# An attention and MLP block on one core: a look-ahead in TensorE's order, and 33 groups of scores on VectorE in place of 34

## The chip, the cores and the metric

The kernel runs on one core of a Trainium2 chip. The metric is the device time of one execution in microseconds. The kernel before takes 461.35 us, the median of three runs (460.85 to 461.57). The profiled execution took 461.18 us; its span from the first to the last instruction is 459.3 us.

## What is computed

Two branches share a layer norm of `x` (2048 rows of 448 values), and their product is added to `x`:

```python
x = A_x
xn = _layernorm(x, axis=-1)
s = _A_ref(xn, A_wqkv, A_wo)          # attention: 16 heads of 28, all 2048 x 2048 scores
g = _silu(_B_ref(xn, B_w1, B_b1, B_w2, B_b2))   # MLP: 448 -> 1792, gelu, -> 448
return x + s * g
```

with the attention's core

```python
scores = jnp.einsum("bhqd,bhkd->bhqk", q, k) * scale
p = _softmax(scores, axis=-1)
o = jnp.einsum("bhqk,bhkd->bhqd", p, v)
```

The softmax needs 16 x 2048 x 2048 exponentials, some 67 million[...]. Most of the kernel is there to keep ScalarE at them.

## The kernel before

**Tiles.** The scores are cut into 1024 tiles of 128 keys by 512 queries of one head. Tile number m belongs to block m // 64 (four heads by 512 queries: 16 blocks) and to head m % 4 of the block. A head's 28 values, padded to 32, fill 32 of the 128 rows of TensorE's array, so up to four score matmuls of different heads run side by side, each in its own row group (`t_score`, L1223). Each writes one PSUM bank of 512 float32 values.

**Units and ScalarE.** ScalarE takes the scores in units: three banks and two banks in turn (two and two in the first block), from the two ends of a ring of banks. `p_scores` makes the scores of unit u once the exp of unit u - 2 has ended (its banks are free then), and `p_exps` (L1279) runs one exp over a unit's banks and writes bfloat16 to slots of a buffer P (18 slots; the page also names them `h` and `xnT`, since in some stretches free parts of these tiles serve as slots). A slot is free once the PV matmuls that read its old content have run.

**Groups on VectorE.** `QUADS` lists groups of four tiles (group q is tiles 4q to 4q + 3) whose exponential VectorE computes in place of ScalarE: four evictions from PSUM as scaled 16-bit integers (`p_apass`, L1382), then five operations over all four tiles that make the powers of two by integer and polynomial arithmetic (`p_expq`, L1433 to L1440). The scores of such tiles are made in banks of their own when one is free, or joined to the matmuls of the next unit (`may_join`, `join`) so that the row groups are filled. Tiles in `QUADS` never reach ScalarE. Their PV work takes twelve matmuls a group where ScalarE's needs four.

**PV and the rest.** `pv_task` (L1494) multiplies eight tiles, and VectorE's groups that are ready, into one accumulator bank; at the end of each block `p_epi` copies it out and divides by the sums. Beside this TensorE has the projections of q, k and v (L744, L1031), the MLP's first product (L1089), its second (L1158), the output product (L1591), and small dummy matmuls (`p_busy`, L905) that keep its clock up when it has little to do. Early in block 9 ScalarE does the GELU in one stretch (L1138) after a change of its table; the exps go on before and after. Later, as the MLP's second product is done chunk by chunk, it takes five tanh for the silu (L1173, L1189).

**What sets the order.** Every engine's order is made before the launch, in Python. All work is split into tasks with an engine, the buffers read and written, a planned length (`dur`, `lat`) and a priority. `run` goes through them as a list scheduler: it works out when each next task could start (`start_of`, from the planned ends of what it needs), takes the one that can start first, and among those of the same engine within 0.1 us of it the one of the best priority. The task is then put at the end of its engine's order, with semaphore waits on what it needs. On the chip each engine runs its list in order. So a task that the planner puts ahead of a unit's scores stays ahead of them on the chip, whatever ScalarE is doing by then. Scores have a priority of 1, other work 1.2 to 6, dummies 95; but a task that can start now is taken before scores that can start in 0.2 us.

The choice in the code before is this:

```python
            s0, p0 = min(cand, key=lambda c: (c[0], c[1][3].prio, c[1][0], c[1][1]))
            E = p0[3].E
            near = [c for c in cand if c[1][3].E == E and c[0] <= s0 + EPS]
            s, p = min(near, key=lambda c: (c[1][3].prio, c[1][0], c[0], c[1][1]))
```

Of the kernel before, what the change touches and what calls it, by code (L numbers as in the profile page):

```python
# [11 lines left out]
PE, ACT, DVE, POOL, SP = ET.PE, ET.Activation, ET.DVE, ET.Pool, ET.SP  # L12
# [15 lines left out]
MTOT = NBLK * T * 4  # L28

GM = 64 * 9 + 6  # L30
QUADS = (17, 22, 25, 36, 37, 59, 65, 72, 82, 87, 99, 103, 115, 122, 129, 135, 138, 142, 152, 153, 157, 158, 164, 168, 178, 180, 194, 199, 211, 213, 222, 229, 234, 242)
SM_SCALE = DH ** -0.5
LOG2E = 1.4426950408889634
EXP_A3, EXP_A2, EXP_LC = 0.16391228, 0.00783292, 1.1187538523466403
# [12 lines left out]
SEM, OWN = 0.07, 0.03  # L47
SWITCH = 0.1
JOINT = 0.05
LEAD, WAIT, GLEAD = 0, 3.0, 48  # L50
EPS = 0.1

# [24 lines left out]
class _Kernel:  # L77
# [132 lines left out]
    def run(self):  # L210
        idle = 0
        while True:
            self.settle()
            if not self.procs:
                return
            cand = []
            for p in self.procs:
                if isinstance(p[3], _Task):
                    s = self.start_of(p[3])
                    if s is not None:  # L220
                        cand.append((s, p))
            if not cand and idle < 100:
                idle += 1
                self.now += 0.1
                continue
            if not cand:
                raise RuntimeError("stuck at %.1f: %s" % (self.now, [(p[0], p[3] if not isinstance(p[3], _Task) else "task") for p in self.procs][:20]))
            s0, p0 = min(cand, key=lambda c: (c[0], c[1][3].prio, c[1][0], c[1][1]))
            E = p0[3].E
            near = [c for c in cand if c[1][3].E == E and c[0] <= s0 + EPS]  # L230
            s, p = min(near, key=lambda c: (c[1][3].prio, c[1][0], c[0], c[1][1]))
            if E == PE and p[3].prio >= 90:
                soon = [c for c in cand if c[1][3].E == PE and c[1][3].prio < 90 and c[0] <= s + p[3].dur]
                if soon:
                    s, p = min(soon, key=lambda c: (c[0], c[1][3].prio))
            idle = 0
            self.now = max(self.now, s)
            self.put(p[3], s)
            self.advance(p)

    def ready(self, toks, ahead=0.0):
        return all(b.tw is not None and b.tw <= self.now + ahead for b in toks)

    def build(self):
        nc = self.nc
        with self.es:
            for E, nm in ((PE, "ev_pe"), (ACT, "ev_act"), (DVE, "ev_dve"), (POOL, "ev_pool"), (SP, "ev_sp")):
                self.evsem[E] = self.sem(nm)
                self.evcnt[E] = 0
            self.alloc()  # L250
            self.schedule()
            block = self.es.enter_context(nc.Block())
            for E, attr in ((SP, "sync"), (POOL, "gpsimd"), (DVE, "vector"), (ACT, "scalar"), (PE, "tensor")):
                lst = self.prog[E]

                def run(eng, lst=lst):
                    for f in lst:
                        f(eng)
                getattr(block, attr)(run)
# [127 lines left out]
    def schedule(self):  # L387
# [27 lines left out]
        K.pv_done = [False] * MTOT  # L415
        K.late = {4 * q + k for q in QUADS for k in range(4)}
        K.late_left = [sum(1 for q in QUADS if K.sub_of(4 * q) == b) for b in range(NBLK + 3)]
        K.late_on = False
# [907 lines left out]
    def may_join(self, r):  # L1326
# [7 lines left out]
        st = K.start_of(p["task"])  # L1334
        return st is not None and max(r["tok"].tr, r["tok"].tw or 0.0) + SEM <= st + JOINT

# [15 lines left out]
    def p_late(self):  # L1352
        K = self
        yield ("until", lambda: K.late_on)
        K.spawn(K.p_room(), 0)
        for q in QUADS:
            m0 = 4 * q
# [49 lines left out]
    def assign(self, ms, b0):  # L1407
        K = self
        n = len(ms)
        runs = [list(range(i, i + n)) for i0, w in K.pon for i in range(i0, i0 + w - n + 1)]  # L1410
        run = min(runs, key=lambda x: (max(K.plast.get(i, -1) for i in x), x[0]))
        for i, m in zip(run, ms):
            K.PB[m] = i
            K.PPREV[m] = K.plast.get(i)
            K.plast[i] = m
        K.units.append((ms, b0, run[0]))
# [266 lines left out]
```

## Time and profile before

| engine | busy, us | share of 459.3 us |
|---|---|---|
| ScalarE | 446.8 | 97% |
| TensorE | 436.3 | 95% |
| VectorE | 373.1 | 81% |
| GpSimd | 40.9 | 9% |

ScalarE's time is made up of these groups (the count, the mean from a record's start to its end, and the sum):

| what | count | mean, ns | busy, us |
|---|---|---|---|
| exp of three banks (1536 columns), into P, `h` or `xnT` | 165 | 1503 to 1518 | 248.9 |
| exp of two banks (1024 columns) | 196 | 1073 to 1099 | 208.1 |
| exp of one bank (512 columns), the last | 1 | 636 | 0.6 |
| GELU of 1024 to 2560 columns | 17 | 1037 to 2333 | 27.3 |
| tanh of 448 to 1792 columns | 5 | 614 to 1766 | 7.2 |

The sums of the first two rows alone are more than the span: records of neighbouring exps overlap, and the page's busy time counts an overlap once. So a record's mean is longer than the time that one more of its kind would add, and the distance between the starts of two neighbours is the better measure of both a price and a delay. The span has four stages: the layer norm and the first projections up to the first exp at 12.9 us, exps up to 247 us, the GELU up to 276 us, exps again up to the start of the last one at 452.2 us, and the end.

### The profile page before, as it was taken

The page shows a single profiled execution, that of the slowest core. Times are in us where ns is not written, and L with a number is a line of the kernel's source. Part 1 is how long each engine was busy: PE and PEld are TensorE (multiplying, and loading weights), DVE is VectorE, ACT ScalarE, POOL GpSimd, SP SyncE. Part 2 cuts the span into 40 slices and gives each one's busy share as a digit, 9 for nine tenths or more (in the row PEclk, how much of TensorE's full clock was granted, in tenths as well). Part 3 has the DMA queues.
Part 4 walks back from the last instruction along what each step waited for, and adds up shares of the span by engine and source line. Part 5 has one row for each costly group of instructions (what it writes and reads, how often), then busy time and mean ns, then how long its engine had stood idle before and what let it go on. Part 6 is the DMA issues. An engine that isn't in the chain of part 4 may idle for free.

```text
span 459.3 us, 10615 instructions
## 1 busy us (share of the span) xinstructions
PE 436.3 (95%) x4431; PEld 162.2 (35%) x4431; DVE 373.1 (81%) x584; ACT 446.8 (97%) x408; POOL 40.9 (9%) x85
## 2 busy tenths in 40 slices
PE   6999999999999999999999999999999999989994
PEld 5543333333332323323333333333323334343452
DVE  8956898894897798878989989847778978999965
ACT  5999999999999999999999999999999999999994
POOL 7470000000000000000000000000000100101111
PEclk9999999999999999999999999999999999999998
DMA  8701000000000000000050000000000001300331
GB/s 269 268 2 37 2 0 1 1 1 4 1 1 0 1 2 3 1 2 1 0 143 1 2 0 2 1 1 0 1 1 2 1 0 42 43 1 1 42 43 41
DMA packets 8050, 11.16 MB, mean 24 GB/s; under 512 B 1698, under 2 KB 6994, under 8 KB 7955
## 3 DMA queue, kind: packets, MB, share of 16 engines
q1 hardware_dynamic: 6850, 8.43, 6.1%
q0 software_dynamic: 864, 1.38, 2.4%
q8 instruction: 35, 0.57, 0.5%
q10 hardware_dynamic: 288, 0.69, 0.4%
q14 instruction: 13, 0.10, 0.1%
HBM read 8.61 MB, written 3.21 MB: 26 GB/s over the span
## 4 chain that ended last, share of the span: by engine, by line
PE 47%; ACT 38%; issue 11%; DVE 3%; POOL 1%; ACTq 0%; DVEq 0%; POOLq 0%
ACT P L1279 18%; PE ring L1223 13%; ACT xnT L1279 9%; ACT h L1279 9%; PE acc L1494 8%; PE ring L1089 5%; PE ring L1158 3%; PE misc L1158 3%; PE acc L905 3%; PE misc L1089 2%; PE misc L744 2%; PE ring L744 2%; PE acc L887 1%; PE misc L1223 1%; PE ring L1031 1%
## 5 line engine op out<-in xcount | busy, mean ns | idle before, releaser
L1279 ACT ACTIVATE P<-ring 128x1024 bf16<-128x1024 f32 (+1 forms) x188 | 217.6, 1265 | 1.4 <-PE ring L1223 1.0
L1223 PE MATMUL ring<-qT,kT 32*128 32x512 bf16 (+2 forms) x1074 | 145.1, 358 | 11.4 <-ACT P L1279 5.6
L1279 ACT ACTIVATE h<-ring 128x1024 bf16<-128x1024 f32 (+1 forms) x102 | 117.8, 1268 | 0.2
L1223 PEld LDWEIGHTS ring<-qT,kT 32*128 32x128 bf16 x1074 | 37.6, 91 | 134.2 <-ACT P L1279 55.7
L1279 ACT ACTIVATE xnT<-ring 128x1536 bf16<-128x1536 f32 (+1 forms) x72 | 83.4, 1308 | 0.0
L1494 PE MATMUL acc<-P,vaug 128*32 128x512 bf16 (+2 forms) x524 | 49.2, 358 | 0.0
L1089 PE MATMUL ring<-xnT,w 128*128 128x512 bf16 x156 | 41.4, 382 | 1.1 <-ACT h L1138 0.9
L1564 POOL CAST rhi<-rc 128x16 bf16<-128x16 f32 x15 | 6.0, 400 | 365.2 <-DVE rc L1562 297.0
L905 PE MATMUL acc<-ident,zero 128*128 128x128 bf16 x393 | 34.3, 221 | 0.0
L1223 PE MATMUL misc<-qT,kT 32*128 32x512 bf16 (+1 forms) x78 | 29.1, 376 | 0.0
L905 PEld LDWEIGHTS acc<-ident,zero 128*128 128x128 bf16 x393 | 22.3, 97 | 18.8 <-issue 18.2
L1494 PE MATMUL acc<-h,vaug 128*32 128x512 bf16 x248 | 27.6, 384 | 0.0
L1158 PE MATMUL misc<-w,h 128*128 128x448 bf16 x112 | 27.3, 356 | 0.0
L1158 PE MATMUL ring<-w,h 128*128 128x448 bf16 x112 | 27.2, 355 | 0.0
L1382 DVE TENSOR_SCALAR x_sb<-misc 128x512 uint16<-128x512 f32 x31 | 21.3, 686 | 6.2 <-PE misc L1223 5.9
L1089 PE MATMUL misc<-xnT,w 128*128 128x512 bf16 x68 | 19.5, 383 | 0.5 <-DVE qT L1581 0.5
L1552 DVE CAST E_sb<-acc 128x512 bf16<-128x512 f32 x15 | 10.4, 690 | 11.7 <-PE acc L1494 11.7
L1494 PE MATMUL acc<-xnT,vaug 128*32 128x512 bf16 (+2 forms) x240 | 18.7, 330 | 0.9 <-ACT P L1279 0.7
L1089 PEld LDWEIGHTS ring<-xnT,w 128*128 128x128 bf16 x156 | 12.1, 97 | 20.0 <-issue 7.2
L1494 PEld LDWEIGHTS acc<-P,vaug 128*32 128x32 bf16 x524 | 11.8, 94 | 15.0 <-issue 11.8
L1382 DVE TENSOR_SCALAR kT<-ring 128x512 uint16<-128x512 f32 x19 | 13.1, 688 | 4.3 <-PE ring L1223 3.4
L1138 ACT ACTIVATE h<-h 128x2048 bf16<-128x2048 bf16 (+2 forms) x8 | 16.2, 2029 | 0.0
(269 smaller groups left out, 663.2 us busy)
## 6 DMA issues: line engine op xcount, KB each, us to landing
w<-in_B_w_dram SPq DMA_DIRECT2D x1, 1568.0 KB, 7.6
w<-in_B_w_dram SPq DMA_DIRECT2D x1, 1344.0 KB, 8.6
out_dram<-in_A_x_dram SPq DMA_DIRECT2D x3, 448.0 KB, 10.7
out_dram<-h POOLq DMA_DIRECT2D x6, 224.0 KB, 3.9
x_sb<-in_A_x_dram SPq DMA_DIRECT2D x2, 448.0 KB, 5.0
h<-in_A_wqkv_dram SPq DMA_DIRECT2D x3, 168.0 KB, 5.1
x_sb<-in_A_x_dram ACTq DMA_DIRECT2D x1, 448.0 KB, 4.4
h<-in_A_x_dram SPq DMA_DIRECT2D x1, 448.0 KB, 4.3
```

What stands on the lines that cost most here:

```text
L744: ins = eng.matmul(bank, w[:, kt, g * 128:(g + 1) * 128], K.xnT[:, kt, c * 512:(c + 1) * 512], start=(kt == 0), stop=(kt == KT - 1))
L887: yield _Task(PE, lambda eng: eng.matmul(bank[:, 0:256], K.ident[:, :], K.E_sb[:, 0, 0:256], start=True, stop=True), [K.b_id, K.b_pads], [ ...
L905: ins = eng.matmul(K.acc[:, 0:128], K.zero[:, :], K.ident[:, :], start=False, stop=True, skip_group_check=True)
L1089: ins = eng.matmul(bank, K.w1[:, kt, ft * 128:(ft + 1) * 128], K.xnT[:, kt, c * 512:(c + 1) * 512], start=(kt == 0), stop=(kt == KT - 1))
L1138: yield _Task(ACT, lambda eng, dst=dst, src=src: eng.activation(dst, src, ACTF.Gelu_apprx_tanh), rd, wr, 0.4267 * n + (0.1 if pc else 0.06 ...
L1158: ins = eng.matmul(ps, hv[:, ft, t * 128:(t + 1) * 128], K.w2[:, ft, :], start=(ft == 0), stop=(ft == FT - 1))
L1223: return eng.matmul(dst, K.kT[32 * j:32 * j + 32, g, t * 128:(t + 1) * 128], K.qT[32 * j:32 * j + 32, g, c * 512 + q0:c * 512 + q0 + nq], ...
L1279: return eng.activation(reg[:, i0:i0 + n, :], K.ring[:, b0:b0 + n, :], ACTF.Exp, scale=SM_SCALE)
L1382: yield _Task(DVE, lambda eng: eng.tensor_scalar(K.unit[u][:, 512 * k:512 * k + 512].bitcast(dt.uint16), bank, SM_SCALE * LOG2E * 128.0, ( ...
L1494: return eng.matmul(K.acc[32 * j:32 * j + 32, q0:q0 + nq], K.vaug[:, t, 4 * g + j, :], ap[:, col:col + nq], tile_position=(0, 32 * j), sta ...
L1552: yield _Task(DVE, lambda eng: eng.tensor_copy(E, K.acc[:, :]), [K.b_acc], [tE], 0.7, 0.0, 0)
L1564: yield _Task(POOL, lambda eng: eng.tensor_copy(K.rhi[:, :], K.rc[:, :]), [K.b_rc], [K.b_rhl], 1.1, 0.0, 1)
```

## The change

The change has two parts. The first is a look-ahead in `run`. While the scores of the next unit are pending, `limit` works out when ScalarE will have finished the exps whose scores are already in TensorE's order, and from it the latest start of the pending scores: this end, less their length, the latency of their result and the planned 0.07 us of a semaphore (`GUARD`, a further reserve, is 0.0). If they can only start later than that, the limit is the time when they can start. A TensorE task other than these scores that could start within 3 us before the limit, but would end after it, is held: it leaves the list of candidates for this choice, unless nothing else were left. In the stretch around the GELU there is no limit. It is for the scores of a unit never to stand behind a task that makes ScalarE wait.

The second part is a new list of groups on VectorE: 33 groups in place of 34, and at other places nearly everywhere. The four tiles of the group that is left out go to ScalarE.

```diff
-QUADS = (17, 22, 25, 36, 37, 59, 65, 72, 82, 87, 99, 103, 115, 122, 129, 135, 138, 142, 152, 153, 157, 158, 164, 168, 178, 180, 194, 199, 211, 213, 222, 229, 234, 242)
+QUADS = (17, 20, 21, 38, 53, 66, 67, 81, 83, 100, 107, 115, 123, 131, 132, 138, 139, 146, 151, 155, 159, 161, 167, 177, 184, 185, 198, 209, 214, 216, 229, 233, 243)
...
+GUARD = 0.0
...
+            lim = self.limit()
+            if lim is not None:
+                held = [c for c in cand if c[1][3].E == PE and c[1][3] is not self.pend["task"] and lim - 3.0 < c[0] < lim
+                        and c[0] + c[1][3].dur + (SWITCH if c[1][3].mode != "row" else 0.0) > lim]
+                cand = [c for c in cand if c not in held] or cand
             s0, p0 = min(cand, key=lambda c: (c[0], c[1][3].prio, c[1][0], c[1][1]))
...
+    def limit(self):
+        if self.pend is None or self.gu is not None and self.exp_u < self.gu + 1 and len(self.units) > self.gu:
+            return None
+        t = self.pend["task"]
+        s = 0.0
+        for b in t.reads:
+            if b.tw is None:
+                return None
+            s = max(s, b.tw + SEM)
+        for b in t.writes:
+            s = max(s, (b.tw or 0.0) + SEM, b.tr + SEM)
+        end = self.tE[ACT] + sum(0.0525 + 0.4267 * len(self.units[v][0]) for v in range(self.exp_u + 1, len(self.units) - 1))
+        lim = end - t.dur - t.lat - SEM - GUARD
+        return lim if s <= lim else s
```

ScalarE's own sequence is otherwise the same but for the places of the tanh; the order on TensorE and VectorE changes nearly everywhere.

## The prediction

> **What bounds the kernel now.** I read the busy shares first, then the groups by shape, then ScalarE's waits, then the order of time around single groups.
>
> ```profile
> PE 436.3 (95%) x4431; PEld 162.2 (35%) x4431; DVE 373.1 (81%) x584; ACT 446.8 (97%) x408; POOL 40.9 (9%) x85
> ```
> ```profile
> L1279 ACT ACTIVATE P<-ring 128x1536 bf16<-128x1536 f32 x85 | 127.8, 1503 | 0.5 <-PE ring L1223 0.2
> L1279 ACT ACTIVATE P<-ring 128x1024 bf16<-128x1024 f32 x102 | 106.7, 1073 | 0.9 <-PE ring L1223 0.8
> ```
> ```profile
> ACT P L1279 <- PE ring L1223: 1.0, 3, 0.5
> ```
>
> ScalarE is busy 97% of the span, and its exps seem to wait for TensorE's scores for 1.0 us in all. That is misleading. A line's mean is start to end, and neighbouring exps overlap: a string of undisturbed ones starts every 1.330 us after a three-bank exp and every 0.903 us after a two-bank one, well under the means of 1503 and 1073 ns. A late exp eats this overlap before any idle time is shown. So I took the 355 pairs of exps that follow each other directly and added up what each start-to-start distance exceeds 1.330 or 0.903 us: **8.2 us**, 6.6 us of it in 40 gaps over 60 ns. One of the largest:
>
> ```profile
> 194.38 0.39 PE L1223 MATMUL ring<-qT,kT 32*128 32x512 bf16 x2
> 194.69 0.40 PE L1494 MATMUL acc<-P,vaug 128*32 128x512 bf16 x3
> ...
> 195.24 0.60 PE L1089 MATMUL ring<-xnT,w 128*128 128x512 bf16 x2
> ...
> 195.78 0.39 PE L1223 MATMUL ring<-qT,kT 32*128 32x512 bf16 x3
> ...
> 196.22 1.45 ACT L1279 ACTIVATE P<-ring 128x1536 bf16<-128x1536 f32 x1 [0.22 <-PE ring L1223]
> ```
>
> The two-bank exp before began at 194.86, so this one was due at 195.76. Its scores (L1223, 195.78) stood behind eight PV matmuls and a two-matmul piece of the MLP's first product (L1089). The exp came 0.44 us after its scores, 0.46 us late; the trace calls 0.22 of that idle. Of the 38 exps over 60 ns late for scores, this distance is 0.43 to 0.46 us in 29 and 0.64 in seven; these seven are all groups to which a fourth tile of the same row group of the array was joined.
>
> So ScalarE bounds the kernel from its first exp at 12.9 us to its last at 452.2. There are two ways to gain: fewer elements for ScalarE, or fewer of these 8.2 us.
>
> **What the Trainium skill says.** "Perfetto Trace Analysis", section "DVE / Act Engine Instruction", says that a ScalarE record ends with the acknowledgement of its writes, while the next instruction may start prefetching earlier; the 1503 ns records every 1330 ns agree. "ScalarE: Activation LUTs", section "What ACT_TABLE_LOAD costs", gives 186 ns plus 0.833 ns an element, less 93 ns of overlap: 946 ns for 1024 elements, where the trace has 903; I use the trace. "TensorE: Matmul & The Clock Gate", "Step-by-step: what each phase is for", says that matmuls stay in program order and only weight loads are pulled ahead; the scores at 195.78 agree, standing behind L1089 although their banks were free.
>
> **The change, part by part.**
>
> *One group of four fewer for VectorE.* It gives ScalarE four more score tiles. In the order of its instructions: three-bank exps 165 to 166, two-bank 196 to 197, and the one-bank exp at the end (0.476 us from its start to the next instruction) is gone. 1.330 + 0.903 - 0.476 = **+1.76 us** on the bounding engine. VectorE loses four evictions (L1382, 0.69 each) and the five operations of one group (three of 0.69, two of 1.22), 7.3 us at 81% busy: worth nothing, since ScalarE's exps hide it. TensorE loses eight PV matmuls and gains 27 dummy matmuls (L905, 393 to 420), which go only where nothing else stands.
>
> *The look-ahead.* It holds back a TensorE task that would end after the last moment at which the pending scores still come in time. Work moves; none vanishes. To see what it can mend, I went through both orders of TensorE's instructions and added up, for every exp, the other work in the two stretches before its scores (after the scores of two exps earlier). Prices: 0.216 us for a 512-wide matmul and 0.189 for a 448-wide one (14 of L1089 take 3.14 us, twelve of L1158 2.38, less their last 0.38), 0.23 for four packed PV matmuls, 0.17 for three dummies. For exps that come due while a two-bank exp runs, and with no other ScalarE work close by:
>
> - 1.65 us and over: 11 exps before, with 2.00 us of gaps; 4 after.
> - 1.45 to 1.65: 36 before, 2.85 us, 16 of them over 60 ns; 32 after.
> - under 1.45: 139 before, 1.77 us; 150 after.
> - Those due while a three-bank exp runs, and those beside other ScalarE work, make up 1.60 us before.
>
> Lower bound of the gain: content alone decides. Then after has 4 x 0.18 + 32 x 0.079 + 150 x 0.0127, and about 1.5 for the rest: 6.7, a gain of **1.55 us**. Upper bound: no work over 1.45 us delays anything any more (about 0.3 us of rounding stays there), the late ones under 1.45 stay, since nothing in the order says why they are late (1.9), and so does 1.2 of the rest, some of it in the first exps, whose content is the same: 3.4, a gain of **4.8 us**. I take **3.5**, a little over the middle. The planner asks for 0.22 + 0.17 + 0.07 = 0.46 us between scores and exp, and the trace has 0.43 to 0.46, so its limit is about right; but its reserve beyond this is zero, and it prices the joined groups that need 0.64 (22 in the order before, 28 after) like the others.
>
> *New waits.* A held task comes later, and PV tasks also free the 18 slots of P that exps write to. In the new order, exp 64 (counted from 0; at 80 us now) writes to slots that a 20-matmul PV task reads, and this task stands behind the scores of that same exp. In the trace of before, such a task holds up exp 259:
>
> ```profile
> 332.23 0.62 PE L1494 MATMUL acc<-P,vaug 128*32 128x512 bf16 x8
> ...
> 333.10 0.39 PE L1494 MATMUL acc<-kT,vaug 128*32 128x512 bf16 x4
> ```
> ```profile
> 333.62 1.02 ACT L1279 ACTIVATE P<-ring 128x1024 bf16<-128x1024 f32 x1
> ```
>
> From its first matmul to the exp it is 1.39 us. Scores can start 0.2 us after an exp's nominal end (0.06 after the recorded one), and the next task 0.32 after them: 0.2 + 0.32 + 1.39 - 0.90 = 1.0 us, less the 0.22 that exp 64 is late now. Exp 282, behind a tanh of 1.59 us, has one piece of L1158 (0.40) more in that chain: 0.2 + 0.32 + 0.40 + 1.39 - 1.59 = 0.7, less the 0.27 of exp 259, which goes. Together **+1.2 us**. Queued behind these exps is all of ScalarE; behind the PV task, the next scores. From both sides: 0.4, if the waits are those of 259; 1.7, if nothing is to be deducted.
>
> *The end.* In the new order the last accumulator copy (L1526) stands behind a product of 0.62 us on VectorE and the last PV task behind seven output matmuls (1.3 us) that start during the last exp (1.33). An estimate from these: **+0.15 us** (0 to 0.6). The rest of the chain after the last exp is the same.
>
> The look-ahead is off in the GELU stage; TensorE's order there differs a little, and ScalarE loses about 0.2 us in it now. I take no change. Held tasks leave TensorE idle for less than 0.3 us at a time between dummies; the clock, 0.997 now, should stay.
>
> Sum: +1.76 - 3.5 + 1.2 + 0.15 = -0.39; 461.35 - 0.39 = **461.0 us**.
>
> **The rivals.**
>
> *The gaps nearly all go.* Gain 4.8, the rest as above: 1.76 - 4.8 + 1.2 + 0.15 = -1.7, so 459.7. For it: the largest gaps have just the pattern that is held back, and the limit agrees with the chip. Against it: 11 late exps had less than 1.45 us of work before them, and 32 places with 1.45 to 1.65 remain.
>
> *The exps cost more than the look-ahead gives.* Gain 1.55: 1.76 - 1.55 + 1.2 + 0.15 = +1.6, so 462.9, slower than before. For it: a reserve of zero, the 0.64 us of joined scores, and two certain costs, more elements on the bounding engine and PV tasks put off until exps wait for slots. Against it: the 11 fullest places shrink to four.
>
> *TensorE becomes the bound.* At 95% busy, held time could push PV and MLP work to the end. Against it: L905 alone is 34 us of filling, and VectorE and TensorE both lose work. I give it no case of its own; it would end with the slower ones.
>
> **How the numbers follow.** 461.0 gets 0.48, 459.7 gets 0.32, 462.9 gets 0.20. Faster by over 0.2% is under 460.43: most of the second case and a fifth of the first, 0.35. Slower by over 0.2% is over 462.27: most of the third, 0.18. The rest, 0.47, is between. The range takes in the first case with its waits at either bound and the middle of both others: 459.4 to 462.7.
>
> **What would show it.** ScalarE's busy time about 448.5 us, with one more record each of the two- and three-bank exps. The sum of start-to-start excess between direct neighbours 5.9 us in place of 8.2, with a gap of about 1 us at exp 64 and 0.7 at exp 282, and few of over 0.1 us elsewhere. Gaps over 60 ns at many places with 1.45 to 1.65 us of work would show the slower case; the two large gaps absent, the faster one. The prediction is wrong as a whole if the GELU stage, the span before the first exp or the 7.1 us after the last one's start moves by more than 0.5 us, or if the clock falls.

## The result, and the profile after

The changed kernel takes **463.06 us** (462.98 to 463.46), the kernel before 461.26 us in the same runs: ratio **1.0041, interval 1.0024 to 1.0059**. It is slower. The prediction was 461.0 us with a range up to 462.7. Its second rival (exps that cost more than the look-ahead gives, 462.9) came near in number, but not by its own sum: it took 1.55 us for the gain of the look-ahead and the other terms as predicted, where the gain turned out larger (2.33) and three of the other terms larger too.

The profiled execution has a span of 461.6 us, 2.30 more than before, at a clock of 0.999. The line of busy times on its page:

```profile
PE 439.6 (95%) x4449; PEld 164.0 (36%) x4449; DVE 368.1 (80%) x575; ACT 447.2 (97%) x409; POOL 41.8 (9%) x85
```

The groups of ScalarE by shape (count, then busy time and mean of one in ns, then idle time before them):

```profile
L1300 ACT ACTIVATE P<-ring 128x1536 bf16<-128x1536 f32 x86 | 133.7, 1554 | 0.9 <-PE acc L1515 0.9
L1300 ACT ACTIVATE P<-ring 128x1024 bf16<-128x1024 f32 x103 | 111.9, 1113 | 0.9 <-PE ring L1244 0.9
```

ScalarE's waits (total, times, longest, us):

```profile
ACT xnT L1300 <- PE acc L1515: 1.0, 1, 1.0
ACT P L1300 <- PE ring L1244: 0.9, 2, 0.5
ACT P L1300 <- PE acc L1515: 0.9, 1, 0.9
```

Lines are 21 further on than before: L1300 is the exp, L1244 the scores, L1515 the PV matmuls, L926 the dummies, L1110 and L1179 the MLP's products. The wait for scores is about what it was; the two rows with L1515, PV matmuls, are new. ScalarE is busy only 0.4 us longer, though its exps are worth 1.76 us more: busy time counts overlapping records once. (In ScalarE's table for the kernel before, it is the sum of all five rows, 492.1 us, that exceeds the span; the first two rows sum to 457.0.) The means of 1554 and 1113 ns are 40 to 51 above those of before, and yet undisturbed exps still start 1.330 and 0.903 us apart. So I use the prediction's measure: an exp is late by what its distance from the start of the one before exceeds these two numbers.

**Why the records are longer.** Call an exp's start plus 1.330 or 0.903 us its nominal end. In a string of exps of which none is late, each record ends some 13 ns later after its nominal end than the one before it. Before, exps 56 to 61 end 0.23 to 0.30 us after it; exp 62 is 0.29 us late, and its own record ends 0.12 us after. In the changed kernel exps 59 to 63 are all on time and end 0.28 to 0.33 us after; exp 64, which is late, 0.12 again. Why this lag grows is not shown. But with fewer late exps it is longer, and what has to wait for an exp's end, and not for the next start, comes later by it. It turns up three times below: at exp 64, ahead of the GELU, and at the end.

| part of the span, us | before | after | difference |
|---|---|---|---|
| up to the first exp's start | 12.94 | 13.20 | +0.26 |
| first to last exp's start: one two-bank exp more | | | +0.90 |
| late exps 64, 259 (before) and 282 (after) | 0.49 | 2.31 | +1.82 |
| all other late exps | 7.73 | 5.40 | -2.33 |
| GELU stage, with the wait ahead of it | | | +0.40 |
| last exp's start to the end: longer exp (1.330 for 0.476) | | | +0.85 |
| rest of the end | | | +0.40 |

The first row is no effect of the change: over the kernels below, whose starts are alike, the first exp begins anywhere between 12.6 and 13.2 us. The rest sums to +2.04; the medians of the timed runs lie 1.80 apart. The 0.90 and the 0.85 are the prediction's prices, put in; that such a price holds is tested below by exps that run twice.

**The look-ahead does its work.** Exp 166, 0.46 us late before behind a PV task and a piece of the MLP, is on time. The timeline of the changed kernel there:

```profile
195.56 0.39 PE L1244 MATMUL ring<-qT,kT 32*128 32x512 bf16 x3
...
196.55 0.60 PE L1515 MATMUL acc<-P,vaug 128*32 128x512 bf16 x7
...
197.09 0.39 PE L1244 MATMUL ring<-qT,kT 32*128 32x512 bf16 x2
197.32 0.37 PE L1244 MATMUL misc<-qT,kT 32*128 32x512 bf16 x1
...
197.73 2.49 ACT L1300 ACTIVATE h<-ring 128x1024 bf16<-128x1024 f32 x2
```

The scores at 195.56 belong to exp 166; between them and the scores before them only a PV task stands. (Exps are compared by their number; the tiles in them differ, since the lists do.) But the next exp, at 197.73, starts 0.64 us after its scores at 197.09, because a fourth matmul of the same row group was joined (197.32), and is 0.18 late. There are 27 such direct neighbours with joined groups after (22 before); together they are late by 1.23 us (0.98).

**What the look-ahead adds.** Exp 64 of the changed kernel, 1.24 us late:

```profile
77.24 1.22 DVE L1461 TENSOR_TENSOR w<-w,x_sb 128x2048 bf16<-128x2048 f16 x1
...
78.22 0.68 PE L926 MATMUL acc<-ident,zero 128*128 128x128 bf16 x9
...
79.07 0.39 PE L1244 MATMUL ring<-qT,kT 32*128 32x512 bf16 x3 [0.18 <-ACT h L1300]
...
79.39 0.61 PE L1515 MATMUL acc<-P,vaug 128*32 128x512 bf16 x8
...
80.84 1.45 ACT L1300 ACTIVATE P<-ring 128x1536 bf16<-128x1536 f32 x1 [0.91 <-PE acc L1515]
```

VectorE's group is ready at 78.46, and TensorE could begin the PV task then. Its order has nine dummies and the scores of exp 64 first. The PV task was held so that these scores come in time; the exp then waits 0.91 us for the slots that the same task frees. At exp 282 the pattern is the same behind a tanh, with the scores of exp 283 ahead of the PV task:

```profile
359.61 0.39 PE L1244 MATMUL ring<-qT,kT 32*128 32x512 bf16 x2
...
360.41 0.61 PE L1515 MATMUL acc<-xnT,vaug 128*32 128x512 bf16 x8
...
361.77 1.45 ACT L1300 ACTIVATE xnT<-ring 128x1536 bf16<-128x1536 f32 x1 [0.95 <-PE acc L1515]
```

It starts 3.56 us after the exp ahead of the tanh, where two other tanh of that width take 2.49: 1.07 us late. All other exps that are over 0.1 us late in the changed kernel start 0.43 to 0.65 us after their own scores, so it is the scores that were late there.

**The end.** The last row of the table is in these lines of the changed kernel:

```profile
453.57 1.50 PE L1612 MATMUL ring<-wo,qT 128*128 128x448 bf16 x7 [0.24 <-ACT xnT L1300]
...
455.00 0.63 PE L1515 MATMUL acc<-xnT,vaug 128*32 128x128 bf16 x32
...
455.40 1.03 POOL L1212 TENSOR_TENSOR h<-w 128x448 bf16<-128x448 bf16 x1 [9.97 <-ACT w L1210]
...
455.89 0.78 DVE L1625 TENSOR_TENSOR h<-h 128x448 bf16<-128x448 bf16 x1
...
456.60 0.94 DVE L1561 RECIPROCAL w<-ring 128x128 f32<-128x128 f32 x1
```

The last PV task stands behind seven output matmuls, and the last reciprocal behind a product (L1625) that takes 0.78 us there in place of 0.39. Besides, the record of the last exp ends 1.65 us after its start, and that of the shorter one before 0.64: 1.01 more, where the prices say 0.85. These 0.16 us are the lag.

### The profile page after: what moved, and what is told of

Read it like the earlier page. It is cut to its first block, busy times and chain, and to the rows that moved or that the text cites. A ratio compares the mean times of both kernels' runs of the same rounds, so it can differ in the third digit from the quotient of the medians.

```text
span 461.6 us, 10637 instructions
## 1 busy us (share of the span) xinstructions
PE 439.6 (95%) x4449; PEld 164.0 (36%) x4449; DVE 368.1 (80%) x575; ACT 447.2 (97%) x409; POOL 41.8 (9%) x85
## 4 chain that ended last, share of the span: by engine, by line
PE 43%; ACT 42%; issue 11%; DVE 3%; POOL 1%; ACTq 0%; DVEq 0%; POOLq 0%
ACT P L1300 21%; PE ring L1244 12%; ACT h L1300 10%; PE acc L1515 8%; ACT xnT L1300 8%; PE ring L1110 6%; PE misc L1179 4%; PE misc L1110 3%; PE acc L926 2%; ACT h L1159 2%; PE ring L765 1%; PE acc L908 1%; PE misc L765 1%; PE ring L1179 1%; PE misc L1595 1%
## 5 line engine op out<-in xcount | busy, mean ns | idle before, releaser
L1300 ACT ACTIVATE P<-ring 128x1024 bf16<-128x1024 f32 (+1 forms) x189 | 220.0, 1314 | 1.8 <-PE ring L1244 0.9
L1244 PE MATMUL ring<-qT,kT 32*128 32x512 bf16 (+2 forms) x1086 | 147.1, 358 | 11.5 <-ACT P L1300 4.1
L1300 ACT ACTIVATE h<-ring 128x1024 bf16<-128x1024 f32 (+1 forms) x102 | 119.1, 1310 | 0.0
L1244 PEld LDWEIGHTS ring<-qT,kT 32*128 32x128 bf16 x1086 | 37.9, 91 | 137.2 <-ACT P L1300 55.5
L1300 ACT ACTIVATE xnT<-ring 128x1536 bf16<-128x1536 f32 (+1 forms) x72 | 83.9, 1319 | 1.0 <-PE acc L1515 1.0
L1515 PE MATMUL acc<-P,vaug 128*32 128x512 bf16 (+2 forms) x528 | 48.8, 358 | 0.0
L1110 PE MATMUL ring<-xnT,w 128*128 128x512 bf16 x160 | 41.9, 382 | 0.7 <-ACT h L1159 0.5
L926 PE MATMUL acc<-ident,zero 128*128 128x128 bf16 x420 | 35.0, 220 | 0.0
L1179 PE MATMUL misc<-w,h 128*128 128x448 bf16 x140 | 33.9, 355 | 0.0
L926 PEld LDWEIGHTS acc<-ident,zero 128*128 128x128 bf16 x420 | 24.1, 98 | 16.5 <-issue 15.0
L1515 PE MATMUL acc<-h,vaug 128*32 128x512 bf16 x248 | 27.4, 384 | 0.0
L1403 DVE TENSOR_SCALAR x_sb<-ring 128x512 uint16<-128x512 f32 x28 | 19.3, 688 | 10.2 <-PE ring L1244 9.9
L1244 PE MATMUL misc<-qT,kT 32*128 32x512 bf16 (+1 forms) x66 | 24.9, 379 | 0.0
L1179 PE MATMUL ring<-w,h 128*128 128x448 bf16 x84 | 20.0, 355 | 0.0
L1110 PEld LDWEIGHTS ring<-xnT,w 128*128 128x128 bf16 x160 | 12.4, 97 | 18.9 <-issue 6.3
L1110 PE MATMUL misc<-xnT,w 128*128 128x512 bf16 x64 | 18.4, 382 | 0.0
L1515 PE MATMUL acc<-xnT,vaug 128*32 128x512 bf16 (+2 forms) x240 | 17.4, 330 | 0.0
L1403 DVE TENSOR_SCALAR x_sb<-misc 128x512 uint16<-128x512 f32 x20 | 13.8, 688 | 4.2 <-PE misc L1244 3.9
L1515 PEld LDWEIGHTS acc<-P,vaug 128*32 128x32 bf16 x528 | 11.7, 95 | 13.1 <-issue 10.0
```

Of the source, the lines that this page charges most:

```text
L926: ins = eng.matmul(K.acc[:, 0:128], K.zero[:, :], K.ident[:, :], start=False, stop=True, skip_group_check=True)
L1110: ins = eng.matmul(bank, K.w1[:, kt, ft * 128:(ft + 1) * 128], K.xnT[:, kt, c * 512:(c + 1) * 512], start=(kt == 0), stop=(kt == KT - 1))
L1179: ins = eng.matmul(ps, hv[:, ft, t * 128:(t + 1) * 128], K.w2[:, ft, :], start=(ft == 0), stop=(ft == FT - 1))
L1244: return eng.matmul(dst, K.kT[32 * j:32 * j + 32, g, t * 128:(t + 1) * 128], K.qT[32 * j:32 * j + 32, g, c * 512 + q0:c * 512 + q0 + nq], ...
L1300: return eng.activation(reg[:, i0:i0 + n, :], K.ring[:, b0:b0 + n, :], ACTF.Exp, scale=SM_SCALE)
L1403: yield _Task(DVE, lambda eng: eng.tensor_scalar(K.unit[u][:, 512 * k:512 * k + 512].bitcast(dt.uint16), bank, SM_SCALE * LOG2E * 128.0, ( ...
```

## The experiments

Two theories are to be told apart. **A**: what counts stands directly ahead: of an exp's scores, or of the PV task that frees its slots. Then single tasks moved should mend single exps. **B**: TensorE's order is full over several exps at a time, and a delay taken from one exp goes to the next unless work leaves the order.

For most runs every engine's order is kept as the planner left it, with the semaphore counts renumbered afterwards, and only listed tasks move:

```diff
+MOVES = ((64, 0, 1),)   # exp, offset from its score task on TensorE, places earlier (negative: later)
+DROPS = ()              # exps; the dummy tasks between the scores of u - 1 and u are left out
```

The dummies feed no output. `MOVES` and `DROPS` are names of these experiments; "late sum" is the sum over all late exps that follow an exp directly.

**Scores of 37 late exps one task earlier, in the kernel before.**

```diff
+MOVES = ((7, 0, 1), (8, 0, 1), (21, 0, 1), (27, 0, 1), (40, 0, 1), (46, 0, 1), (62, 0, 1), (68, 0, 1),
...
```

> The kernel before with its own 34 groups and all orders frozen, but for TensorE: the scores of 37 units whose exps were over 60 ns late are put one task earlier. No look-ahead, no other change. Theory A (tasks ahead of the scores make the exps late, and TensorE has room to wait): the 5.9 us of these 37 gaps go nearly all, 8.2 us becomes about 3.5, and the kernel takes 456.5 to 457.5 us. Theory B (TensorE is too full; a task put behind the scores makes the next ones late): the sum of gaps stays over 6.5 us and the time within 1 us of 461.3.

464.92 us, ratio 1.0086 (1.0072 to 1.01). The late sum rose from 8.22 to 12.33 us. Exp 40 came in time (343 ns late before), and exp 42 was 409 late; 62 came in time, and 64 went from 217 to 652. Neither number that was expected came true, and the loss is larger than B's; its direction is B's: work moved behind a unit's scores stands ahead of the next ones. Slots are not what they wait for: of the exps over 0.1 us late, all but 9 and 259 start 0.43 to 0.64 us after their scores (exp 9 went from 117 to 803 ns late, for a PV task).

**Exp 64 in the kernel before: scores ahead of the PV task.**

```diff
+MOVES = ((64, 0, 1),)
```

> The kernel before with one swap in TensorE's order: the scores of exp 64 go ahead of the 20-matmul PV task that frees the slots this exp writes to. Theory A (holding a PV task back for scores whose own exp needs that PV task is what cost at exp 64): exp 64 is 1.1 to 1.3 us late in place of 0.22, and the time rises by about 1.0 us, to 462.3. Theory C (the wait at exp 64 in the changed kernel comes from its list of groups, whose last group VectorE finishes late): exp 64 stays 0.2 to 0.4 late and the time doesn't change.

461.80 us, ratio 1.0016 (1.001 to 1.0023). Exp 64 went from 217 to 1031 ns late, and no other exp changed by over 30 ns. This one exchange costs 0.8 us, with the old list of groups; so C (the list makes the wait) isn't needed for it.

**The opposite in the changed kernel.**

```diff
+MOVES = ((64, 0, -1),)
```

> The changed kernel with one swap in TensorE's order: the scores of exp 64 go behind the PV task that frees its slots, in the place where the planner without look-ahead would have them. Theory A: exp 64 is 0.5 to 0.7 us late in place of 1.24, the time falls by 0.6 us, to 462.4. Theory C: the PV task waits for VectorE's group where it stands, exp 64 stays over 1.0 late.

462.49 us, ratio to before 1.0032 (1.002 to 1.0045). Exp 64 fell from 1237 to 851 ns late, the rest stayed: 0.39 us, less than the 0.5 to 0.7 expected. The PV task still stood behind the nine dummies; what they cost is read below, where they are left out.

**And exp 282.**

```diff
+MOVES = ((64, 0, -1), (283, 2, 1))
```

> As a64, and the PV task that exp 282 needs goes ahead of a two-matmul piece of the MLP's second product (0.4 us). Theory A: exp 282 is 0.6 to 0.8 us late in place of 1.07; the rest of it is VectorE's group, ready about 0.5 us after the scores before. Time 462.0 to 462.2. Theory C: exp 282 stays at 1.0 to 1.1, since VectorE's group ends at 359.9 us and sets when the PV task can start.

462.38 us, ratio 1.003 (1.0019 to 1.0042). Exp 282 came 0.36 us earlier after the exp ahead of the tanh (0.71 late for 1.07, as expected), but exps 284 and 288 became 189 and 115 ns late, which they had not been: the medians differ by 0.1 us, within the noise. Most of a local mend was passed on.

**Ten tasks of dummies out of the kernel before.**

```diff
+DROPS = (46, 62, 64, 98, 198, 332)
```

> The kernel before with every engine's order kept as it is, but without ten tasks of dummy matmuls on TensorE (30 matmuls) that stand between the scores of exps u - 1 and u at six late exps (46, 62, 64, 98, 198 and 332: late by 111, 285, 217, 208, 130 and 98 ns, 1.05 us together). Theory B (a place in TensorE's order is too full, and a delay moves on to a later exp unless work leaves the order): here work leaves it, so most of the 1.05 us goes, the late sum falls from 8.2 to about 7.3 us, and the time to about 460.1 us (ratio 0.998). Theory A (only what stands directly ahead of the scores counts, the dummies fill idle time): the six exps stay late by about as much, ratio 1.000.

461.11 us, ratio 1.0003 (0.9995 to 1.0011). Exps 46, 62, 98 and 198 came within 60 ns, 64 fell from 217 to 137, 332 stayed at 97; but 68 rose from 135 to 345, and 48 and 110 became 66 and 103 late. The late sum fell by 0.38 us, where 0.9 was expected, and the timed runs don't show even that. Work that leaves the order helps, but less than its own place suggests.

**The same with eight scores moved**, those which passed nothing on in the first run.

```diff
+MOVES = ((136, 0, 1), (166, 0, 1), (264, 0, 1), (274, 0, 1), (298, 0, 1), (308, 0, 1), (310, 0, 1), (348, 0, 1))
+DROPS = (46, 62, 64, 98, 198, 332)
```

> As the run without ten tasks of dummies, and also the scores of eight late exps (136, 166, 264, 274, 298, 308, 310, 348) go one task earlier on TensorE: those of the 37 of the first run of moved scores that did not pass their delay on to the next exps. If delays are local, that is, if a move that passed nothing on there passes nothing on when made without the others, these eight give about 1 us more: about 459.0 us, ratio 0.995 to 0.996, late sum about 6.3 us. If a move's effect depends on the others around it, new late exps appear and the ratio is that of the run of drops alone, or above it.

**460.11 us, ratio 0.9982 (0.9976 to 0.9989)**: faster than both kernels, though not the 459.0 of purely local delays. The late sum is 7.31 us. All eight exps came in time (1.45 us), but 168, 170, 281, 314, 352 and 353 took some 0.8 of it: a move that passed nothing on among 36 others did so here.

**The price of a tile on ScalarE.** Three exps of the kernel before run twice:

```diff
+TWICE = (99, 101, 103)
...
+                if u0 in TWICE:
+                    eng.activation(K.wv[:, :, :].rearrange("p k n -> p (k n)")[:, 0:1024].rearrange("p (b n) -> p b n", b=2), K.ring[:, b0:b0 + n, :], ACTF.Exp, scale=SM_SCALE)
                 return eng.activation(reg[:, i0:i0 + n, :], K.ring[:, b0:b0 + n, :], ACTF.Exp, scale=SM_SCALE)
```

> The price of a tile on ScalarE, by itself. The kernel before, every order kept, with three two-bank exps of the order (units 99, 101 and 103) executed a second time at once, into a part of a buffer that is no longer read: 3 x 0.903 = 2.71 us more work for ScalarE, none elsewhere. If ScalarE bounds the kernel and the distance of starts is the price, the time grows by 2.7 us less what late exps near there give back (0.1 to 0.3): 463.6 us, ratio 1.0055. If TensorE's order sets the pace, it grows by under 1.5 us.

463.69 us, ratio 1.006 (1.0047 to 1.0072): +2.74 us for 2.71 of work. The distance of starts is the price, and ScalarE bounds the kernel around these exps (99 to 103). The late sum, 8.23 us, was as before.

**The end of the changed kernel.**

```diff
+                blocks.insert(i - 1, blocks.pop(i))                       # TensorE: last PV task one earlier
+                blocks[-7:-2] = [blocks[-6], blocks[-7], blocks[-4], blocks[-3], blocks[-5]]   # VectorE
```

> The changed kernel with the two moves of before (PV tasks for exps 64 and 282) and a third at the end: the last PV task goes one task earlier on TensorE, and VectorE takes the last copy, the reciprocal and the products of the output in the order of the kernel before. If the 0.40 us by which the end grew beyond its longer last exp comes from this order, the stretch from the last exp's start to the end falls from 8.37 to about 7.95 us, and the time to about 462.0 (ratio to before 1.002). If it comes from the last exp's size, the stretch stays at 8.3 to 8.4 us.

462.21 us, ratio 1.003 (1.0019 to 1.004). The last exp's start to the end fell from 8.37 to 8.19 us: 0.09 from the PV task and 0.10 from the product that stood ahead of the reciprocal. So 0.18 of the 0.40 is shown to come from the order. In what is left, some 0.2, the trace shows two things: the 0.16 of lag in the last exp's end, and a reciprocal that starts 1.09 us after the last PV task (0.88 before), as another product (0.63 us on VectorE, from 454.76) ends. That order was not tried.

**Dummies out further ahead of late exps.**

```diff
+DROPS = (46, 62, 64, 98, 198, 332, 38, 140, 141, 162, 164, 179, 186, 330, 331)
```

> As the run with ten tasks of dummies out and eight scores moved (460.11 us), but with fourteen more dummy tasks out of TensorE's order, in the stretches two to six exps ahead of those that were still late there: 40, 144, 168, 180, 190 and 332 (342, 156, 267, 207, 165 and 97 ns). If a late exp is the sum of what TensorE has to do over several exps (the delay was passed on because nothing between could yield), taking filling out further ahead takes at least half of these 1.23 us: about 459.4 us, late sum 6.6 us or less. If only the task directly ahead of the scores counts, these six stay as they are: 460.1 us.

464.67 us, ratio 1.0073 (1.0059 to 1.0087). The edit takes out more than was said: eighteen tasks more, not fourteen (TensorE has 309 dummy matmuls in L905's place, after 393 and then 363). The busy time by stretch tells why it is slower. A line has the stretch and its length, the busy time and number of instructions of PE, PEld, DVE, ACT and POOL, the granted clock, and the share and rate of DMA:

```profile
48.00:50.00 2.00, 1.23 (x12) 0.31 (x10) 0.86 (x2) 1.84 (x2) 0.41 (x2) 0.70 0.00 0
50.00:51.00 1.00, 1.00 (x5) 0.16 (x4) 0.84 (x2) 0.95 (x1) 0.00 (x0) 0.50 0.00 0
...
56.00:57.00 1.00, 1.00 (x47) 0.68 (x44) 0.92 (x2) 1.00 (x2) 0.00 (x0) 1.00 0.00 0
```

and the timeline of the same kernel:

```profile
48.98 0.61 PE L1266 MATMUL ring<-qT,kT 32*128 32x512 bf16 x3 [0.77 <-DVE rc L1606]
...
54.78 1.45 ACT L1323 ACTIVATE h<-ring 128x1536 bf16<-128x1536 f32 x1 [2.20 <-PE ring L1266]
```

TensorE now idles 0.77 us up to 48.98, where five dummy tasks had stood. From 48.79 to 55.61 its granted clock is 0.50, and exp 40 came 2.3 us late. The same happened once more, where four had stood (0.78 us idle, 194.21 to 194.99; clock 0.50 from 195.56 to 198.97; exps 165 and 166 late by 1.03 and 0.45). Of the six exps aimed at, 40 and 168 lie just behind these falls and tell nothing; of the other four (144, 180, 190, 332) only 180 gained (207 to 125). So taking filling out further ahead did little where it can be read, and these dummies are not idle filling: they hold the clock.

**Exp 64's dummies and the GELU stage of the changed kernel.**

```diff
+MOVES = ((64, 0, -1), (283, 2, 1), (213, -13, -3))
+DROPS = (64,)
```

(with the two edits at the end from the run above)

> The changed kernel with the moves at exps 64 and 282 and at the end, and two edits more: the three dummy tasks that stand between the scores of 63 and the PV task that frees the slots of exp 64 are out, and in the GELU stage the last score matmul of a VectorE group goes behind three pieces (six matmuls) of the MLP's first product, which it holds up. If the 0.85 us that exp 64 is still late is that PV task behind the dummies, it falls to 0.3 to 0.55 (the VectorE group that the task reads is ready only shortly before). If the 0.30 us that the last GELU waits is the held-up first product, the stretch from table load to table load falls by 0.2 to 0.3 us. Together about 461.6 us, ratio to before 1.0015. If neither, 462.2.

462.68 us, ratio 1.0037 (1.0023 to 1.005). At exp 64 the expectation held: 851 to 535 ns late, so the dummies cost 0.32 us. Now the PV task waits for VectorE's group:

```profile
78.18 0.61 PE L1564 MATMUL acc<-P,vaug 128*32 128x512 bf16 x8 [0.22 <-DVE w L1510]
...
79.82 1.45 ACT L1349 ACTIVATE P<-ring 128x1536 bf16<-128x1536 f32 x1 [0.21 <-PE ring L1292]
```

(L1349 is the exp, L1564 the PV matmuls in this kernel.) The GELU stage stayed at 26.85 us from table load to table load: the score matmul broke the MLP's product at another place, but broke it all the same. And VectorE got its scores later, so that the PV task after the GELU started after 0.87 us of idle time; exps 215, 216 and 218 came 250, 297 and 109 ns late.

**The score matmul beside its neighbour.** In the kernel before, two score matmuls go side by side at 261.69 us, in different row groups; in the changed kernel the same two stand apart:

```profile
263.73 0.38 PE L1244 MATMUL misc<-qT,kT 32*128 32x512 bf16 x1
264.39 0.60 PE L1110 MATMUL ring<-xnT,w 128*128 128x512 bf16 x2 [0.28 <-ACT h L1159]
264.93 0.38 PE L1244 MATMUL ring<-qT,kT 32*128 32x512 bf16 x1
265.25 2.76 PE L1110 MATMUL ring<-xnT,w 128*128 128x512 bf16 x12
...
274.13 2.65 ACT L1159 ACTIVATE h<-ring 128x1536 bf16<-128x1536 f32 x2
276.80 1.28 ACT L1163 ACT_TABLE_LOAD   x1
```

Joined again in the changed kernel, and without the move of the run before:

```diff
+MOVES = ((64, 0, -1), (283, 2, 1), (213, -27, 1))
+DROPS = (64,)
```

> The changed kernel with the moves at exps 64 and 282, at the end, and without the three dummy tasks ahead of exp 64's PV task (as in the run before, but without its move in the GELU stage); and a score matmul of a VectorE group in that stage goes one task earlier, so that it runs side by side with the score matmul of the same group and the MLP's first product is broken once less. If that break is what the GELU stage lost, table load to table load falls from 26.84 to about 26.55 us and the time, with the 0.3 us at exp 64, to about 461.6 us. If not: 26.84 and 461.9.

461.74 us, ratio 1.002 (1.0012 to 1.0029), and 26.59 us from load to load. The timeline of this kernel (L1292 scores, L1158 the MLP's product):

```profile
262.57 0.38 PE L1292 MATMUL misc<-qT,kT 32*128 32x512 bf16 x1
262.75 0.38 PE L1292 MATMUL ring<-qT,kT 32*128 32x512 bf16 x1
263.24 3.32 PE L1158 MATMUL ring<-xnT,w 128*128 128x512 bf16 x14
...
272.97 2.41 ACT L1207 ACTIVATE h<-ring 128x1536 bf16<-128x1536 f32 x2
275.39 1.28 ACT L1211 ACT_TABLE_LOAD   x1
```

The last two GELUs take 2.41 us in place of 2.65: the second no longer waits for the product.

**The opposite in the kernel before.**

```diff
+MOVES = ((211, -28, -1),)
```

> The opposite in the kernel before: one of the two score matmuls that go side by side at 261.69 us in the GELU stage goes one task (two matmuls of the MLP's first product) later, nothing else. If a break costs 0.3 us there, table load to table load grows from 26.59 to about 26.85 us, and the time by 0.2 to 0.3 us, to about 461.3. If the stage has room for it, both stay.

461.35 us, ratio 1.0009 (1.0001 to 1.0018); load to load grew from 26.59 to 26.85 us. Both ways it is 0.26 us, for one break of the product by a lone score matmul. It is the whole difference between the loads. The other 0.15 us of the stage lies ahead of the first of them: in every kernel here this load starts 17 to 19 ns after the record of the exp before it ends, and that record is 1.72 us long in the changed kernel, 1.57 before. It is the lag again.

**Each part alone.** First the look-ahead with the old list:

```diff
-QUADS = (17, 20, 21, 38, 53, 66, 67, 81, ...
+QUADS = (17, 22, 25, 36, 37, 59, 65, 72, ...
```

> One part of the change alone: the look-ahead with the 34 groups of before. In its order eight exps (9, 64, 88, 210, 238, 239, 259, 260) have their scores ahead of the PV task that frees their slots, where before has two (9, 259) and the changed kernel four (9, 64, 282, 283). If the look-ahead's price is such waits, this kernel is slower than before by about 1 us for each new one and by more where the PV task itself waits: 466 us or more, although its other exps are seldom late for scores. If the two parts add up (look-ahead a gain of 2 to 3.5 us, list a cost of 1.8), it is at 458 to 459.5 us.

494.77 us, ratio 1.0732 (1.0713 to 1.0752). ScalarE's waits in it:

```profile
ACT xnT L1300 <- PE acc L1515: 14.8, 1, 14.8
ACT w L1194 <- DVE w L1184: 13.6, 2, 12.8
```

Then the new list without the look-ahead (the code before with another list):

```diff
-QUADS = (17, 22, 25, 36, 37, 59, 65, 72, ...
+QUADS = (17, 20, 21, 38, 53, 66, 67, 81, ...
```

> The other part alone: the 33 groups of the changed kernel, planned without the look-ahead. In its order six exps (9, 64, 180, 181, 282, 283) have their scores ahead of the PV task that frees their slots. If a list of groups is fitted to the way of choosing it was made with, this is slower than both kernels: over 466 us, with a few long waits for slots and about as many exps late for scores as before. If the parts add up, it is before plus the price of one group less: 463.1 us.

483.22 us, ratio 1.0482 (1.0462 to 1.0501), with these waits:

```profile
ACT P L1279 <- PE acc L1494: 7.5, 2, 5.5
ACT xnT L1279 <- PE acc L1494: 5.4, 1, 5.4
```

The parts don't add. With the old list exps 64 and 88 are late by 1.24 and 1.21 us, as much as exp 64 of the changed kernel; then one tanh waits 12.8 us for VectorE and exp 238 14.8 us for a PV task. Its late sum is 8.4 us, these two included. In the other run exps 64, 180 and 282 wait for slots (2.2, 5.7 and 5.5 us), and the other late exps sum to 12.9 us. The GELU stage is 2.4 to 2.8 us longer in both (29.41 and 29.02 us from load to load). A list of groups is fitted to one way of choosing, it seems; neither number is the worth of a part, and what each is worth in the changed kernel stays open.

Of the two theories, A holds for the PV task of exp 64: one exchange costs 0.8 us and mends in part. B holds for the scores of the kernel before, but not wholly: the eight moves passed on about half of what they mended, and still gained.

## Why the prediction was wrong

**What bounds the kernel, and the price of the exps: right.** Repeated exps cost 2.74 us for 2.71. The +1.76 us itself stands in the table by the same prices (0.90 and 0.85) and was not measured alone. The prediction's 448.5 us of busy time was wrong (447.2), by the very overlap that it had warned of.

**The look-ahead: mis-sized, 3.5 predicted and 2.33 measured**, inside its bounds of 1.55 and 4.8. By the prediction's own classes (before, then after; exp 64 is in the second row before and left out after):

| work ahead of the scores | exps | late, us | expected to remain |
|---|---|---|---|
| 1.65 us and over | 11, then 4 | 2.00, 0.58 | 0.3 to 3.25 with the next row |
| 1.45 to 1.65 | 36, then 32 | 2.85, 1.02 | |
| under 1.45 | 139, then 149 | 1.77, 2.29 | 1.9 |
| others | 169, then 170 | 1.60, 1.51 | 1.2 to 1.5 |

The full places did what was hoped: 1.60 us remain of 4.85, near the middle of their bounds, and 0.57 of it is exp 8 alone. (The two sums shown with the prices of a matmul give 0.212 and 0.182 us; the starts of these matmuls lie 0.216 and 0.190 apart, so the prices used were right.) Two steps failed. "The late ones under 1.45 stay": they grew by 0.5, and over two fifths of what is still late is in places that the content of two stretches calls harmless. Exps 18, 40, 90, 278 and 328 are such places, late by 186 to 303 ns. The joined groups don't explain it: in this row they are late by 0.92 us before (18 of them) and 0.90 after (16). The runs with moved scores show in the kernel before how it may come about: the delay of a moved task goes to later exps. For the changed kernel this is argued from those runs and not shown; none of its own late places but 64 and 282 was mended singly. The other step is arithmetic: the 8.2 us from which 3.5 were taken hold the 0.22 of exp 64 and the 0.27 of exp 259, and both were deducted again from the new waits. Of the 1.17 us by which this term missed, up to 0.49 is that.

**New waits: mis-sized, +1.2 predicted and +1.82 measured.** The places and the mechanism were right, and the exchanges at exp 64 show it in both directions. The term that failed is "scores can start 0.2 us after an exp's nominal end": they started 0.37 (exp 64) and 0.49 us (exp 282) after it. At exp 64 they followed the recorded end by 0.05 us, as the prediction has it (0.06), but this end came 0.31 us after the nominal one, by the lag. At exp 282 the scores ahead of the PV task stood behind four matmuls of the MLP (L1179, from 358.75). The other terms were near: 1.45 and 1.36 us from the first PV matmul to the exp for 1.39, and 0.48 for the 0.40 of the MLP's piece.

**The GELU stage: "I take no change" was wrong, +0.40 us.** The orders were read as differing a little; the difference between the table loads was one pair of score matmuls parted, 0.26 us by both runs. The other 0.15 is a table load that comes 0.41 us after it is due (0.26 before), since it follows the end of an exp whose record is that much longer.

**The end: +0.15 predicted, +0.40 measured.** The two causes named account for 0.18, by the run that mended the end. A further 0.16 is the later end of the last exp, which the prediction had left out.

The four terms missed by 1.17, 0.62, 0.40 and 0.25 us, 2.44 together and all to the same side. The range let one term at a time go to its bound; and it does not, as the prediction says, take in the middle of both rivals, since 462.9 lies above 462.7. Against a time measured to 0.2%, the small terms that were set at nothing or near it mattered as much as the large one. The slower rival got a chance of 0.20. Of its reasons ("a reserve of zero, the 0.64 us of joined scores, and two certain costs") the two costs were there, joined scores are 0.25 us, and a larger reserve was not tried; that its number came out near is in part luck.

With exps 64 and 282, the end and the GELU stage mended as far as they were, the changed kernel is still 0.2% slower than before (461.74 for 460.95 us): the four tiles more on ScalarE cost 1.76 us by their price, and the 2.33 us of the look-ahead pay for them, but not for what came with it.

## What to carry to other kernels

A look-ahead that guards one wait has to know the others: a task that is held back so that scores come in time may be the task that frees what the same exp writes to, and holding it cost 0.8 us at one place here. On an engine that is 95% busy, moving work passes a delay on; only a few moves, picked by what earlier moves had passed on, together with work taken out, gave a gain (0.18%). And where an order decides the time, any place where the two orders differ can have a price; 0.26 us here came from one pair of matmuls parted.

## What the runs showed of the hardware

- The granted clock changed on a grid. In each of the 16 traces its changes lie whole multiples of 3.413 us apart; in the run with more dummies out it fell at 48.79 and 195.56 us and rose at 55.61 and 198.97. The Trainium skill, "TensorE: Matmul & The Clock Gate", section "What's actually happening", says that the clock follows TensorE's activity in free-running windows of some 3.4 us, and that fits. Busy time in such a window does not say when it falls:

```profile
45.37:48.79 3.42, 2.40 (x30) 0.66 (x18) 3.09 (x6) 3.42 (x4) 0.00 (x0) 1.00 0.00 0
192.15:195.56 3.41, 2.22 (x47) 0.81 (x44) 3.23 (x5) 3.41 (x4) 0.00 (x0) 1.00 0.00 0
```
```profile
121.27:124.68 3.41, 2.02 (x13) 0.59 (x13) 2.09 (x4) 3.41 (x4) 0.00 (x0) 1.00 0.02 5
```

  The first two windows are of the run with more dummies out (TensorE 70% and 65% busy), and the clock fell after both. The third is of the run with repeated exps (59% busy), and it did not fall; there it also stayed at 1.00 over an idle stretch of 1.00 us (127.13 to 128.13). What does separate them is work by area: count a matmul as its rows times columns over 128 x 128, times its width over 512, so a quarter for a 512-wide score or PV matmul and for a 128-wide dummy. In all traces together 2121 windows have the full clock, up to the last fall. The 18 after which it fell hold at most 5.96 such full matmuls, the other 2103 at least 6.10; the three above 5.96, 4.99 and 6.25. In the half-clock stretches of the run with more dummies out it stayed after a window with 5.05 and rose after 6.67 and 7.06. This is inferred from the traces afterwards, no run was made for it, and some matmul records may be missing. It says why dummies matter: the five tasks ahead of 48.98 come to 3.75. The same page's section "HAM oscillation — how this bites in real kernels" speaks of idle gaps of over 3.4 us as what to avoid; here the falls came with gaps of 0.77 and 0.78.
- In six kernels with the end of before, the stretch from the last exp's start to the end took 7.09 to 7.15 us; in the two where the clock had fallen before the last matmul (the run with ten tasks of dummies out and the one with more out) 7.31 and 7.34.
- The mean record of a three-bank exp into P was 1501 to 1521 ns in the kernel before and those made from it with single tasks moved or left out, and 1552 to 1556 in the changed kernel and those made from it in the same way, with the same distance between undisturbed starts in both. A record's end lags by some 13 ns more with each exp on time, up to 0.39 us, and by 0.12 after a late one; the price doesn't follow.
- A product on VectorE of 0.39 us took 0.78 us beside a product on GpSimd (455.89 and 455.40), the same in all three kernels with that order, and 0.38 us in the run where it stood after it. The Trainium skill, "GPSIMD Engine Reference", section "Specifications", says that GpSimd shares its interfaces to SBUF with VectorE and that VectorE's instructions with two inputs there, or in a two-port mode, contend with it. This is one place that agrees.
